# A 2D Fourier transform and a two-layer MLP on one core: loads, tables and low halves as pieces of the written-out order, and the folding of later batches on VectorE

## The chip, the cores and the metric

One NeuronCore of a Trainium2 chip runs the kernel as one program. The metric is the device time of an execution in microseconds. TensorE (PE) multiplies matrices, VectorE (DVE), ScalarE (ACT) and GpSimd (POOL) work element by element, SyncE (SP) issues most of the DMA transfers. Each engine takes its own instructions in order; semaphores join them.

## The reference

The input x has 8 batches of 3008 rows with 256 features. Of each batch the 2D Fourier transform is taken, and its real part goes, row by row, through a two-layer MLP:

```
X = np.fft.fft(np.fft.fft(x, axis=1), axis=2).real        # x: (8, 3008, 256)
h = X.reshape(24064, 256) @ w_in                          # w_in: (256, 2048)
r = np.maximum(h, 0.0)
out = (s * (r * r) + b) @ w_out                           # w_out: (2048, 256)
```

## The kernel before

**What is computed where.** The transform over the features is a matrix on the features, so it is multiplied into w_in once, at the start (`fold_w_in`, pieces "w"). The transform over the 3008 rows is a real transform with many symmetries. Rows that lie symmetrically are added and subtracted first (folding, `load_first`, `load_second` for batch 0, `load` for the others); what remains are eight small sums per batch half, which TensorE makes with cosine and sine tables `dft_sb` (`transform`, L573), and VectorE joins into the spectrum. The spectrum of a batch has 3 blocks of 502 columns.

**Precision.** TensorE's fast format keeps fewer bits, so operands are split into a high part and a low rest: the spectrum into `spec_h` and `spec_l`, the weights into `wd_h`/`wd_l` and `wo_h`/`wo_l`, the activations into `gh` and `gl`. A product is three matmuls (high x high, high x low, low x high).

**A step** is one block of a batch with one of 16 slices of the 2048 hidden features; there are 8 x 3 x 16 = 384. `first_layer` (a piece "L"): six matmuls into two PSUM banks `ab` (L646), three VectorE operations that read them (L651, L654, L655) and make `h`, then relu, square and the cast to `gh` on ScalarE (L656, L657, L666). The low half `gl` = h - gh (L669) is the second part of the same generator (a piece "G"): GpSimd makes it, for some steps of the first block VectorE. `second_layer` (a piece "S"): twelve matmuls on `gh` and `gl` into four banks `po` (L679). After the 16th S of a block, `finish` turns the four banks into results (L696) and stores them. The banks `ab` are four, and the transform takes its PSUM from the same four; `h`, `gh` and `gl` have three buffers each.

**The order is written out by hand.** Two strings of letters say in which order pieces of work are emitted; `_in_order` then ties the instructions of PE, DVE, ACT and POOL to just this order. SP isn't tied, but it also takes its DMA issues in the order of emission. START covers batch 0 and the first 54 S, BATCH is run for each later batch. Letters: "x", "y" fold batch 0; "s", "u" are its transform, phase 0 and 1, in 11 pieces each; "l" folds the next batch, 8 chunks of five operations, one operation a piece (L504, L506, L508, L510, L512); "v", "o" are the next batch's transform; "r" loads a piece of the weights, "a", "b", "e", "f" decode it; "n", "m" are the one feature that stands apart; "t" loads tables. In the pieces of "v", v1 to v7 hold in turn: the first `lf`, matmuls, joining, matmuls, joining, `uv` (L385, L386), the second `lf` (L388, L389, L367); v8 holds the matmuls that need it, v9 to v11 joining, matmuls and joining.

**Before, around the change.** The x tiles of batch 0, the feature table `feat` and two pieces of the weights are issued ahead of the order, in the sequence of LOADS ("xxfxxxwxwxx"); the tables `dft_sb` are issued through GpSimd's own queue (L727). All folding of batches 1 to 7 runs on GpSimd (`LOADS_ON_GPSIMD` names all eight chunks). In BATCH an "L" emits its `gl` at once, and in START "G" is a letter of its own:

```
if what == "L" and step < NB * NBLK * NJ:
    first()
    next(lows.pop(0))
```

The functions that the change touches, and those that call them:

Of the kernel before, what the change touches and what calls it, by code (L numbers as in the profile page):

```python
# [15 lines left out]
P = 128  # L16
NB, S, D, FF = 8, 3008, 256, 2048
# [4 lines left out]
G = 24  # L22
# [12 lines left out]
SPLIT = 754  # L35

LOWS_OF_STEPS_ON_VECTOR = (0, 1, 2, 3, 4, 7, 8, 10, 11, 12, 14)
LOWS_ON_VECTOR = (5,)  # L40
Y_ON_VECTOR = (0, 1, 2, 5)
X_ON_VECTOR = (0, 1, 2, 3, 5, 6, 7)
LOADS_ON_GPSIMD = (0, 1, 2, 3, 4, 5, 6, 7)
SUMS_ON_SCALAR = ()
LOADS = "xxfxxxwxwxx"
WORDS = (
    ("in", 0, 0), ("in", 0, 1), ("in", 1, 0), ("in", 1, 1), ("out", 0), ("out", 1), ("in", 2, 0), ("out", 2),
    ("in", 2, 1), ("out", 3), ("in", 3, 0), ("out", 4), ("in", 3, 1), ("out", 5), ("out", 6), ("out", 7),
)
START = (  # L50
# [7 lines left out]
)  # L58
BATCH = (
# [3 lines left out]
)  # L63

def _unit(num, den):
# [141 lines left out]
def _lay_out_x(x):  # L218

    rows, swap = _rows()
    padded = np.zeros((NB, S + 1, D), np.float32)
    padded[:, :S] = x
    first = np.arange(P)
    second = np.concatenate([[0], D - np.arange(1, P)])
    order = np.stack([np.concatenate([first, second]), np.concatenate([second, first])])
    xq = np.ascontiguousarray(padded[:, rows[..., None], order[swap]])
    xn = np.ascontiguousarray(padded[:, rows, P].transpose(1, 2, 3, 0))  # L230
    return xq, xn

def _in_order(tc):
# [14 lines left out]
def kernel(ctx: ExitStack, tc: tile.TileContext, xq, xn, dft, turn, feat, w_in, w_out, s, b, out):  # L250
    nc = tc.nc
# [4 lines left out]
    stage = ctx.enter_context(tc.tile_pool(name="stage", bufs=2))  # L256
# [4 lines left out]
    act = ctx.enter_context(tc.tile_pool(name="act", bufs=3))  # L261
# [14 lines left out]
    feat_sb = const.tile([P, 2, 2 * P], F32, name="feat_sb")  # L276
# [17 lines left out]
    def load_words(part, pool, tag):  # L294
        raw = pool.tile([P, 512, 2], I32, name="raw", tag=tag)
        src = words(part)
        nc.sync.dma_start(raw.rearrange("p (j d) t -> p j (d t)", j=src.shape[1]), src)
        return raw
# [401 lines left out]
                nc.sync.dma_start(out[su, blk, :, 2 * pm:2 * pm + 2], o)  # L700

    room = spec.tile([P, 2 * NT], F32, name="room", tag="spec_h")
    t_ny = room[:R, 256:512].rearrange("p (c q b) -> p c q b", c=8, q=4)
    nc.sync.dma_start(t_ny, xn)
    nc.sync.dma_start(turn_sb, turn)  # L710
    folded[0] = spare.tile([P, 2, 8, 2 * P], F32, name="cs")
    tiles, raws = [], []
    for what in LOADS:
        if what == "x":
            pool, tag = ((stage, "xt"), (act, "gl"), (act, "gh"))[(len(tiles) + 1) // 3]
            tiles.append(pool.tile([R, 4, D], F32, name="xt", tag=tag))
            nc.sync.dma_start(tiles[-1], xq[0, :, len(tiles) - 1])
        elif what == "w":
            raws.append(load_words(WORDS[len(raws)], act, "h"))
        else:  # L720
            nc.sync.dma_start(feat_sb, feat.rearrange("c p d -> p c d"))
    nc.sync.dma_start(sb_s, s.partition_broadcast(P))
    nc.sync.dma_start(sb_b, b.partition_broadcast(P))

    def tables():
        for ph, leaves in ((0, slice(0, 4)), (0, slice(4, 8)), (1, slice(0, 8))):
            nc.gpsimd.dma_start(dft_sb[:, ph, :, leaves], dft[:, ph, :, leaves])  # L727
            yield

    def load_weights():  # L730
        for part in WORDS[2:]:
            raws.append(load_words(part, stage, "xt"))
            yield

    decoding = []
# [22 lines left out]
    pending, lows = [], []  # L758
# [20 lines left out]
    def second():  # L779
# [6 lines left out]
            finish(su, blk, po)  # L786

    work = {
        "t": tables(), "x": load_first(tiles), "y": load_second(tiles), "r": load_weights(), "a": begin_weights(),
        "b": go_on(), "e": go_on(), "f": go_on(), "w": fold_weights(),  # L790
        "n": nyquist(0, t_ny, room), "m": nyquist(1, t_ny, room),
        "s": transform(0, 0), "u": transform(0, 1), "l": load(1),
# [13 lines left out]
    while step < NB * NBLK * NJ:  # L806
        work = {}
        if su < NB - 1:
            work = {"l": load(su + 1), "v": transform(su + 1, 0), "o": transform(su + 1, 1)}
        for what in BATCH.split():  # L810
            if what == "L" and step < NB * NBLK * NJ:
                first()
                next(lows.pop(0))
            elif what == "S" and pending:
                second()
            elif what in work:
                next(work[what])
        su += 1
    while pending:
        second()  # L820
    _in_order(tc)
# [32 lines left out]
```

## Time and profile before

| | |
|---|---|
| runs | 1632.76, 1634.05, 1635.02 us; median 1634.05 us |
| profiled execution | 1632.94 us, span of its instructions 1631.2 us |
| mean granted TensorE clock | 0.986 of 2.4 GHz |
| GpSimd busy | 1143.4 us, 70% of the span, 842 instructions |
| transfers | 67.41 MB, mean 41 GB/s |
| steps of the two layers | 384, with 1536 x 3 matmuls at L679 and 768 x 3 at L646 |

The profile is of one execution. Matmuls are pipelined, so the mean length of one (0.38 us) is longer than the distance at which they start (0.21 us). A wait is put down to the instruction that came last. The body of the run repeats once per batch.

### The profile page before, as it was taken

How to read it: one execution, taken by the hardware profiler on the slowest of the kernel's cores; microseconds unless marked ns; L12 is line 12 of the kernel's file. 1: busy time of each engine (PE TensorE's matmuls, PEld its weight loads, DVE VectorE, ACT ScalarE, POOL GpSimd, SP SyncE). 2: the span in 40 equal slices, each digit the busy share in tenths (PEclk: the TensorE clock that was granted, in tenths of full speed). 3: DMA queues.
4: the chain of work that ended last, by engine and by line, in shares of the span. 5: the costliest groups of instructions: out<-in, count | busy, mean ns of one | idle time of the engine just before them, and what ended most of it. 6: DMA issues, size and time to landing. Idle time of an engine off the chain costs nothing.

```text
span 1631.2 us, 21931 instructions
## 1 busy us (share of the span) xinstructions
PE 1573.0 (96%) x7526; PEld 1384.5 (85%) x7526; DVE 1128.8 (69%) x1738; ACT 1234.5 (76%) x1311; POOL 1143.4 (70%) x842
## 2 busy tenths in 40 slices
PE   3889999999999999999999999999999999999998
PEld 2568888888888888888888888888888888888887
DVE  7898658757775577756776658765777557775563
ACT  2688687786777778787787877878677777878776
POOL 4647785698557976589766895669855797655554
PEclk8899999999999999999999999999999999999999
DMA  6311110021000210002100110002100021000000
GB/s 177 104 56 61 44 57 10 23 71 45 26 33 17 65 58 4 33 26 65 51 8 26 62 46 35 8 26 71 46 26 32 17 65 42 1 32 8 26 26 26
DMA packets 25316, 67.41 MB, mean 41 GB/s; under 512 B 4915, under 2 KB 9875, under 8 KB 25206
## 3 DMA queue, kind: packets, MB, share of 16 engines
q1 hardware_dynamic: 24934, 64.83, 12.5%
q0 software_dynamic: 272, 1.18, 0.3%
q8 instruction: 60, 0.98, 0.3%
q14 instruction: 50, 0.41, 0.1%
HBM read 41.27 MB, written 24.73 MB: 40 GB/s over the span
## 4 chain that ended last, share of the span: by engine, by line
PE 86%; DVE 8%; ACT 2%; issue 1%; DMA 1%; POOL 1%; SPq 0%; ACTq 0%; DVEq 0%; POOLq 0%
PE po L679 55%; PE ab L646 28%; PE ab L573 3%; DVE uv L385 1%; DVE even L651 1%; DVE lf L388 1%; DVE h L654 1%; DVE h L655 1%; DMA xt<-in_xq 1%; ACT h L657 0%; ACT h L656 0%; DVE uv L386 0%; DVE lf L377 0%; PE ab L338 0%; DMA wny<-wny_dram 0%
## 5 line engine op out<-in xcount | busy, mean ns | idle before, releaser
L669 POOL TENSOR_TENSOR gl<-h,gh 128x1004 fp32r<-128x1004 f32 x373 | 804.7, 2159 | 395.4 <-ACT gh L666 334.7
L656 ACT ACTIVATE h<-h 128x1004 f32<-128x1004 f32 x384 | 398.5, 1038 | 264.7 <-DVE h L655 260.2
L651 DVE SCALAR_TENSOR_TENSOR even<-ebc,wny,ab 128x502 f32<-128x502 f32 x384 | 282.4, 736 | 376.9 <-PE ab L646 358.2
L679 PE MATMUL po<-gh,wo_h 128*128 128x502 f32 (+1 forms) x1536 | 456.6, 379 | 1.5 <-ACT gh L666 1.1
L679 PE MATMUL po<-gh,wo_l 128*128 128x502 f32 (+1 forms) x1536 | 453.1, 377 | 1.3 <-DVE wo_l L273 1.3
L666 ACT CAST gh<-h 128x1004 fp32r<-128x1004 f32 x384 | 395.3, 1029 | 56.6 <-PE po L679 45.5
L657 ACT ACTIVATE h<-h 128x1004 f32<-128x1004 f32 x384 | 399.8, 1041 | 12.2
L679 PE MATMUL po<-gl,wo_h 128*128 128x502 f32 (+1 forms) x1536 | 388.4, 375 | 2.8 <-DVE gl L669 2.8
L679 PEld LDWEIGHTS po<-gh,wo_l 128*128 128x128 f32 x1536 | 292.1, 190 | 37.4 <-DVE wo_l L273 1.6
L679 PEld LDWEIGHTS po<-gh,wo_h 128*128 128x128 f32 x1536 | 290.4, 190 | 38.6 <-issue 1.9
L679 PEld LDWEIGHTS po<-gl,wo_h 128*128 128x128 f32 x1536 | 290.6, 189 | 38.2 <-DVE gl L669 3.2
L654 DVE TENSOR_TENSOR h<-even,ab 128x502 f32<-128x502 f32 x384 | 260.2, 678 | 77.8 <-POOL gl L669 27.3
L646 PE MATMUL ab<-spec_h,wd_h 128*128 128x502 f32 x768 | 296.1, 386 | 8.4 <-DVE even L651 6.5
L646 PE MATMUL ab<-spec_l,wd_h 128*128 128x502 f32 x768 | 291.2, 379 | 0.0
L646 PE MATMUL ab<-spec_h,wd_l 128*128 128x502 f32 x768 | 289.9, 377 | 0.0
L655 DVE TENSOR_TENSOR h<-even,ab 128x502 f32<-128x502 f32 x384 | 257.9, 671 | 0.0
L646 PEld LDWEIGHTS ab<-spec_h,wd_h 128*128 128x128 f32 x768 | 145.7, 190 | 33.1 <-DVE even L651 9.1
L646 PEld LDWEIGHTS ab<-spec_h,wd_l 128*128 128x128 f32 x768 | 146.6, 191 | 18.1
L646 PEld LDWEIGHTS ab<-spec_l,wd_h 128*128 128x128 f32 x768 | 146.0, 190 | 17.8 <-issue 0.8
L696 DVE TENSOR_SCALAR o<-po,sb_s,bias 128x502 f32<-128x502 f32 x94 | 68.7, 793 | 12.4 <-PE po L679 12.3
L561 POOL TENSOR_TENSOR spec_l<-o,spec_h 128x368 fp32r<-128x368 f32 (+3 forms) x80 | 61.6, 791 | 18.1 <-ACT spec_h L559 14.7
L573 PEld LDWEIGHTS ab<-dft_sb,lf 96*128 96x128 f32 x384 | 51.4, 195 | 25.3 <-DVE lf L388 20.1
(94 smaller groups left out, 819.3 us busy)
## 6 DMA issues: line engine op xcount, KB each, us to landing
xt<-in_xq SPq DMA_DIRECT2D x64, 384.0 KB
out<-o SPq DMA_DIRECT2D x46, 502.0 KB
raw<-in_w_in SPq DMA_DIRECT2D x8, 512.0 KB
raw<-in_w_out SPq DMA_DIRECT2D x8, 512.0 KB
ebc<-e_dram SPq DMA_DIRECT2D x16, 251.0 KB
ebc<-e_dram SPq DMA_DIRECT2D x8, 126.0 KB
out<-o SPq DMA_DIRECT2D x4, 251.0 KB
ebc<-e_dram SPq DMA_DIRECT2D x8, 125.0 KB
```

The lines of the kernel that those rows point to most:

```text
L561: nc.gpsimd.tensor_sub(lo, src, hi.bitcast(F32))
L573: nc.tensor.matmul(ps[:, kind, i], src[:, i, kind * P:(kind + 1) * P], dft_sb[:, ph, kind, leaf + i], start=True, stop=True,)
L646: nc.tensor.matmul(beside(ps[kind]), w[:, kind, fj], in_turn(m[:, kind]), start=i == 0, stop=i == 2)
L651: nc.vector.scalar_tensor_tensor(beside(even), in_turn(ebc), wny[:, j:j + 1], beside(ps[0]), op0=ALU.mult, op1=ALU.add)
L654: sub(h[:, 1], even, ps[1])
L655: add(h[:, 0], even, ps[1])
L656: nc.scalar.activation(h, h, AF.Relu)
L657: nc.scalar.activation(h, h, AF.Square)
L666: nc.scalar.copy(gh_halves, h)
L669: engine.tensor_sub(gl_halves, h, gh_halves.bitcast(F32))
L679: nc.tensor.matmul(beside(po[2 * pm + dh][:, :n]), l[:, j, dh * P:(dh + 1) * P], in_turn(r[:, pm])[:, :n // 2], start=start and i in (0, 2 ...
L696: nc.vector.tensor_scalar(o[:, dh], po[2 * pm + dh][:, :NT], *args, ALU.mult, ALU.add)
```

## The change

The loads of batch 0 and of the constants become pieces ("X", "c"), as the tables ("t") already were. The tables go through SyncE's queue. All 16 pieces of weights are loaded by "r". In BATCH, "G" is now a letter of its own, as in START; what is left of the low halves is emitted after the last batch's string. `LOADS_ON_GPSIMD` is empty, so `load` takes VectorE for all chunks of batches 1 to 7. START and BATCH are written anew.

```diff
-LOADS_ON_GPSIMD = (0, 1, 2, 3, 4, 5, 6, 7)
+LOADS_ON_GPSIMD = ()
-LOADS = "xxfxxxwxwxx"
...
 START = (
-    "t t x a r n y x r x x x s y n y b n x x s y x y s s a x s e s f b s s e a u t s a b e f w s r s b u u y e a f "
-    "y r b f w w w w a e y f L b r r e a u L a G b r L e b r e f G a L b G a f e b w r S S f S r f u w w w L G e a "
-    "a m L G b b e S e f S L r a L r G r b e G m f m a L r u S f L G L G G S L S b u e a S S G u f u w b f w w e u "
-    "u a G f S L L b G e S G f L L S l L l G G S L l l l G L S l l G S L l G L l G S G l L G S L S l S l L l l G l "
-    "S L S L l S L G S G S l G l L l L G G l l l l G S L S v G L S L l l G L l l G S l l S l l S L L G S L l l L l "
-    "S G l L G S G l L G G v l l S v l L S G L S S L S v G l v S G v v L L S o G L v G o G v G S L S L v G S v L o "
-    "S G L o L G o G S L S S L L G S G G o L S G G L L S L S S G o o G G o o o S"
+    "X X n X X x X X r X y t X x y x a r x t y r x x r c s s a b e x b t x x e a f n b s e f w r y s s w f n s s a "
+    "a s u u b e s b u e y r y a s f s b w e w f w r a L y y r b a L r G L e b e f r G S a L b e G f f G u c S u f "
+    "r S w w w a b w a m L S L r m u b e e G f a L G r L b e G a S f S f L r L b G G m e r f a G L S b e r u S w w "
+    "u w f a u a L u L b G e b u S f G L e S S f L S G G L L G l S L l G G S L S S l L L S l l G S L l G G S l L S "
+    "l L G l S l G G l l l L l l S L G S G l G L l l l S L G G l S l L S l G l L l L v S v G S l v l L S G l L G L "
+    "G l G l l S L l S S L L l S l L S L l G L l l v S v l l l G L l G S G S S G o S v L G L G v G G S L L G S S v "
+    "G o v L v o S G L S v o L S o G L G L G o S S S G L L S S o G L G G L S o o S L G L G G S L G o S o"
 )
 BATCH = (
-    "l l L S S S l l L L S l l l L l L S l L L l S l L l S L l l S l S L L l l S L l l L l S S l l l L l L l S l S "
-    "S S L v l S l l L l S L l L v S L l l l l l v l S l v S l v L l L S L S L v v L S S v v L S L L S v L S S S o "
-    "L S v L L o S o L S o L S o L S L L o S L S L L o S S S o L S o L S L L S S L L S o L S o L S S"
+    "l l L G S l S S l l L G L G G l S l L l l l L S G l L G S G l l l L G l l S L l G l L S l l L S l S G L G L l "
+    "S S G l L v G L v l l S L S G l G L l l S l L S G l L G v l S G L S l L G v l l l G L S G G v S l S l L S l l "
+    "l v L G v S L G S L S L S G v L G G S L G S v L o S o G L o v G v S G L S G L L S L o G o L S o S L G L o S G "
+    "S L L S G G G L o S G G S G o S L L S S L L S L G o G G G S o L S L G L S S G S G"
 )
...
-    for what in LOADS:
-        if what == "x":
-            pool, tag = ((stage, "xt"), (act, "gl"), (act, "gh"))[(len(tiles) + 1) // 3]
+
+    def load_x():
+        for c in range(8):
+            pool, tag = ((stage, "xt"), (act, "gl"), (act, "gh"))[(c + 1) // 3]
             tiles.append(pool.tile([R, 4, D], F32, name="xt", tag=tag))
-            nc.sync.dma_start(tiles[-1], xq[0, :, len(tiles) - 1])
-        elif what == "w":
-            raws.append(load_words(WORDS[len(raws)], act, "h"))
-        else:
-            nc.sync.dma_start(feat_sb, feat.rearrange("c p d -> p c d"))
-    nc.sync.dma_start(sb_s, s.partition_broadcast(P))
-    nc.sync.dma_start(sb_b, b.partition_broadcast(P))
+            nc.sync.dma_start(tiles[-1], xq[0, :, c])
+            yield
+
+    def load_constants():
+        nc.sync.dma_start(feat_sb, feat.rearrange("c p d -> p c d"))
+        yield
+        nc.sync.dma_start(sb_s, s.partition_broadcast(P))
+        nc.sync.dma_start(sb_b, b.partition_broadcast(P))
+        yield
 
     def tables():
         for ph, leaves in ((0, slice(0, 4)), (0, slice(4, 8)), (1, slice(0, 8))):
-            nc.gpsimd.dma_start(dft_sb[:, ph, :, leaves], dft[:, ph, :, leaves])
+            nc.sync.dma_start(dft_sb[:, ph, :, leaves], dft[:, ph, :, leaves])
             yield
 
     def load_weights():
-        for part in WORDS[2:]:
-            raws.append(load_words(part, stage, "xt"))
+        for i, part in enumerate(WORDS):
+            raws.append(load_words(part, *((stage, "xt") if i > 1 else (act, "h"))))
             yield
...
             if what == "L" and step < NB * NBLK * NJ:
                 first()
+            elif what == "G" and lows:
                 next(lows.pop(0))
...
         su += 1
+    for low in lows:
+        next(low)
     while pending:
         second()
```

## Rows read from the trace of the kernel before

**Rows 1.** The page, busy time by engine: us, share of the span, instructions.
```profile
PE 1573.0 (96%) x7526; PEld 1384.5 (85%) x7526; DVE 1128.8 (69%) x1738; ACT 1234.5 (76%) x1311; POOL 1143.4 (70%) x842
```

**Rows 2.** Windows: length; PE, PEld, DVE, ACT, POOL busy us; clock; DMA share, GB/s.
```profile
0.00:10.00 10.00, 0.00 (x0) 0.00 (x0) 3.95 (x11) 1.28 (x1) 4.34 (x15) 1.00 0.79 199
10.00:20.00 10.00, 2.01 (x5) 0.69 (x6) 7.96 (x18) 1.95 (x7) 4.78 (x11) 1.00 1.03 290
400.00:420.00 20.00, 18.35 (x87) 15.87 (x86) 19.28 (x25) 12.84 (x14) 11.74 (x7) 0.91 0.20 72
1075.00:1174.00 99.00, 99.00 (x477) 88.42 (x476) 59.58 (x92) 76.93 (x78) 86.12 (x68) 1.00 0.15 44
1075.00:1268.00 193.00, 191.31 (x925) 170.51 (x924) 132.44 (x204) 149.50 (x154) 142.50 (x98) 0.99 0.12 37
1180.00:1200.00 20.00, 18.88 (x88) 16.57 (x89) 17.48 (x27) 14.41 (x16) 10.19 (x7) 0.91 0.13 53
```

**Rows 3.** Waits of VectorE to 150 us: us in total, times, longest.
```profile
DVE xt L521 <- DMA xt<-in_xq: 7.8, 2, 5.9
DVE even L651 <- DMA wny<-wny_dram: 4.6, 2, 2.4
```

**Rows 4.** Operations on `uv` from 400 us: count, ns min/median/max, first and last start.
```profile
L385 DVE TENSOR_TENSOR uv<-cs x6: 3612/3626/3655, 400.2 to 1368.5; 96x512 f32<-96x512 f32 x6
L386 DVE TENSOR_TENSOR uv<-cs x6: 674/676/677, 403.8 to 1372.0; 96x512 f32<-96x512 f32 x6
```

**Rows 5.** Timeline near 400 us: start, us, operation, idle time before it.
```profile
399.04 4.25 POOL L669 TENSOR_TENSOR gl<-h,gh 128x1004 fp32r<-128x1004 f32 x2
...
400.23 3.61 DVE L385 TENSOR_TENSOR uv<-cs 96x512 f32<-96x512 f32 x1
...
404.04 2.40 POOL L669 TENSOR_TENSOR gl<-h,gh 128x1004 fp32r<-128x1004 f32 x1 [0.75 <-ACT gh L666]
...
404.36 2.35 DVE L388 TENSOR_TENSOR lf<-uv 96x256 f32<-96x256 f32 x1
406.64 0.41 DVE L389 TENSOR_TENSOR lf<-uv 96x256 f32<-96x256 f32 x1
...
406.77 1.24 PE L573 MATMUL ab<-dft_sb,lf 96*128 96x96 f32 x8 [1.65 <-DVE lf L388]
```

**Rows 6.** Waits of TensorE from 260 us on.
```profile
PE ab L573 <- DVE lf L388: 10.0, 6, 1.7
```

**Rows 7.** Timeline near 193 us.
```profile
193.28 5.81 DVE L377 TENSOR_TENSOR lf<-cs 96x256 f32<-96x256 f32 x1
...
194.60 4.22 POOL L669 TENSOR_TENSOR gl<-h,gh 128x1004 fp32r<-128x1004 f32 x2
...
199.80 0.78 PE L646 MATMUL ab<-spec_h,wd_h 128*128 128x502 f32 x1 [2.97 <-DVE even L651]
```

**Rows 8.** Lines of VectorE, 1075 to 1268 us: count, busy us, mean ns.
```profile
L651 DVE SCALAR_TENSOR_TENSOR even<-ebc,wny,ab 128x502 f32<-128x502 f32 x48 | 35.3, 735 | 48.7 <-PE ab L646 46.9
...
L655 DVE TENSOR_TENSOR h<-even,ab 128x502 f32<-128x502 f32 x48 | 32.2, 672 | 0.0
L696 DVE TENSOR_SCALAR o<-po,sb_s,bias 128x502 f32<-128x502 f32 x12 | 8.8, 793 | 0.4 <-PE po L679 0.4
```

**Rows 9.** Lines of GpSimd in the same stretch.
```profile
L504 POOL TENSOR_TENSOR xt<-xt 96x512 f32<-96x512 f32 x8 | 10.4, 1302 | 0.0
...
L506 POOL TENSOR_TENSOR xt<-xt 96x256 f32<-96x256 f32 x8 | 5.9, 732 | 0.4
```

**Rows 10.** The chain of waits near 222 us: start, us, what.
```profile
222.18 2.54 PE po L679 x12
224.72 1.27 PE ab L646 x6
```

**Rows 11.** Lines of ScalarE from 1075 to 1268 us.
```profile
L657 ACT ACTIVATE h<-h 128x1004 f32<-128x1004 f32 x48 | 50.0, 1041 | 1.5
```

**Rows 12.** Timeline of VectorE in the opening.
```profile
6.97 0.28 DVE L407 TENSOR_TENSOR room<-room 96x128 f32<-96x128 f32 x1
```

More of the change, by code (lines that the diff above doesn't have):

```diff
@@ L788 @@
     work = {
-        "t": tables(), "x": load_first(tiles), "y": load_second(tiles), "r": load_weights(), "a": begin_weights(),
+        "X": load_x(), "c": load_constants(), "t": tables(), "x": load_first(tiles), "y": load_second(tiles), "r": load_weights(), "a": begin_weights(),
         "b": go_on(), "e": go_on(), "f": go_on(), "w": fold_weights(),
```

## The prediction

> **What bounds the kernel now.** I read the page first: TensorE is busy for 1573 of 1631.2 us, the next engine, ScalarE, for 76% [rows 1]. So only time in which TensorE stands, or runs at half clock, can be won. Windows of 10 and 20 us, and then the waits, show three places that hold it.
>
> The opening: in the first 10 us TensorE does nothing, in the next 10 it works 2.01 us [rows 2], and while VectorE folds batch 0, rebuilds the weights and feeds the first steps, it is filled unevenly until about 140 us. VectorE is the engine without air there; its two largest waits, for x and for `wny`, sum to 12.4 us, of which 5.9 is the landing of the first x [rows 3].
>
> One stall per batch: at 406.77 TensorE waits 1.65 us for `lf` L388. Upstream, `uv` L385 needs 3.61 us and ends just after a pair of `gl` does (399.04 + 4.25 = 403.29), though its twin L386 needs 0.68. L388 takes 2.35 us, against 0.41 for L389 with the same shape, and again ends with a `gl` (404.04 + 2.40) [rows 4, 5]. It repeats: the six L385 from 400.2 to 1368.5 us lie 193.7 us apart and all take 3.6 us [rows 4], and TensorE waits for L388 six times, 10.0 us in all [rows 6]. Behind four of the six the granted clock falls as well, to 0.91 over 20 us, 1.8 us each; the rows of the first and the last of them stand for the four [rows 2].
>
> One hold near 193 us: `lf` L377, of the shape that takes 0.41 us when free, takes 5.81. It starts while GpSimd folds and ends after two `gl` that follow without a gap (194.60 + 4.22 = 198.82). TensorE waits 2.97 us behind it, and its next matmul lasts 0.78 us, against 0.38 at full clock [rows 7].
>
> So a VectorE operation with two SBUF inputs doesn't run beside a GpSimd operation: it waits for its end, and for the next one's if that follows at once. Those with an input in PSUM (L651, L655) keep their length [rows 8].
>
> The Trainium skill says this in "SBUF — State Buffer", "SBUF: two separate sides": the pair of ports that VectorE and GpSimd share is an exclusive lock, held for a whole instruction, also against a VectorE operation with two SBUF inputs. The trace agrees for one instruction and goes beyond it in L377, which was held through several. It speaks against this change, as all 280 moved operations are of that kind; the time by it is rival 2.
>
> **The change part by part.**
>
> *Folding batches 1 to 7 on VectorE.* A batch has 8 chunks of 5 operations. GpSimd loses 10.4 us for L504 and about 5.9 us for each of the four like L506, 34 us a batch [rows 9]. VectorE gets 8 x (0.68 + 4 x 0.41) = 18.5 us, by the free L386 and L389 [rows 4, 5].
>
> Has VectorE room? I add up the new BATCH from its start to its 23rd S, which covers all 40 `l` and v1 to v7. VectorE: 23 L of 0.735 + 2 x 0.672 = 2.08 us, 47.8; one group of results, 4 x 0.79 = 3.2; the 13 operations of the v pieces at 0.41 to 0.68, 6.3; the folds, 18.5; in all 75.8 us [rows 8]. TensorE: 23 x (1.27 + 2.54) = 87.6 us, its two small groups of the transform left out [rows 10]. So 11.8 us are free for holds. The 40 `l` stand in 26 runs with an L between them or a v, so each run may be held 0.45 us on average before VectorE sets the pace. Before, GpSimd was busy for 86.1 of 99 us in this stretch and VectorE for 59.6 [rows 2]: the load is turned round, with a lower peak.
>
> How long will a run be held? From nothing to a whole `gl`, 2.13 us (half of the pair's 4.25) [rows 5]. I take 0.2, by the phase: ScalarE needs 3 x 1.04 = 3.1 us between the last `h` of a step and its `gl` [rows 11], and most `l` stand directly behind an L, when the step's own `gl` can't have begun. The `gl` of the step before ends 3.1 + 2.13 us behind its own `h`, and a step is 3.81 us, so at most 1.42 us of it are left when VectorE is punctual, and less the later VectorE is. With 26 x 0.2 = 5 us this half holds 81 of 88 us: free for TensorE, which has a lead of 3 to 5 steps. I add 2 us over the run for single collisions (0 to 12).
>
> *The stalls that go.* The new order puts four S and three L between v7, which makes `lf`, and v8, which needs it: 14.0 us, where the old one has two S and one L, 6.4 us [rows 10]. And GpSimd, without the folds, seldom has two operations back to back. Gain 6 x 1.65 + 4 x 1.8 = 17.1 us; from 8, if a hold of `lf` merely shrinks, to all of it. Late next would be the PSUM bank that v2 holds until v3, now over four L in place of one: an L then finds three banks, and VectorE must have read the first half of the step before within some 3 us. At its load that holds.
>
> The hold near 193: gone with the folds on GpSimd, 2.97 us and, as behind the other stalls, about 1.7 of clock: 4.7 us (0 to 4.7).
>
> *The price in START.* Batch 1 is folded beside the late opening. From S28 to S36 the new START gives VectorE 10 L (20.8), 16 `l` (7.4), v3 and v5 (2.2) and a group of results (3.2), 33.6 us, and TensorE 8 x 2.54 + 10 x 1.27 = 33.0. No room there; a lead of 4 to 5 steps takes some 4 us of lag. I take +3 (0 to 10).
>
> *Loads and tables as pieces, tables through SyncE.* SyncE's queue now holds x ahead of everything, and feat, the tables and most weights later. VectorE's second wait for x, 7.8 - 5.9 = 1.9 us [rows 3], came with feat and two tables ahead of or beside the third x. And n now stands ahead of the first fold, so that 0.5 us of its work (L407, 0.28, and the smaller L408) falls into the first 5.9 [rows 12]. New on SyncE are three table issues. The first stands behind seven x and a word, 3.4 MB: at the 290 GB/s of the second 10 us [rows 2] through by some 14 us, while `s1` has 13 us of VectorE's work ahead of it behind the first landing, so about 19. feat and the third table stand behind a word that waits for the slot of the second x, freed early, by y2. GpSimd loses three issues in an opening where it is busy for less than half [rows 2]: 0, and if that cover were gone, what they took of it. Gain 2.4 (from -6, if SyncE's line runs late, to 6.5, the two waits without the first landing).
>
> *The rest of the opening.* By S13 either order has given VectorE the same pieces, so another sequence moves only its waits; 0.6, within the bounds just given.
>
> *G as pieces in BATCH.* GpSimd keeps only `gl` and `spec_l`, 142.5 - 34 = 108.5 of 193 us [rows 2], and takes them as they come. 0; were that cover gone, a `gl` behind two `spec_l` is under 2 us late, inside the lead.
>
> Sum, from the profiled execution's 1632.9 us (span 1631.2; 1.1 under the runs' median 1634.05): -17.1 - 4.7 - 3.0 + 2 + 3 = -19.8, so 1613; on the median's level 1614.
>
> **Rivals.**
>
> 1. *The stall changes place.* Holds of `uv`, `o`, `lf` and the folds still cost TensorE a stop in each batch, and the clock with it. For: `gl` alone was what L385 and L388 sat behind at 400 us, and `gl` remains. Against: the 14 us between v7 and v8. If all 17.1 us come back, 1634 - 3 - 4.7 + 5 = 1631; with half of them 1623.
>
> 2. *VectorE becomes the bound of the folding half (slower).* Each run of `l` meets a running `gl`, and GpSimd takes the port again between runs. It decides from 0.45 us of hold per run on, in six batches and, with as many runs, in START. At 0.6 us: 26 x 0.15 x 7 = 27 us, 1641; at 0.9: 82 us, 1696. The worst, a whole `gl` for each run, is 26 x 1.68 x 7 = 306 us. For: all six L385 were held 2.9 us. Against: they met two `gl` in a row behind a GpSimd that had folded until then, and L386 and L389, second in their run, weren't held at all [rows 4, 5].
> The skill's page named above gives the same end: whoever comes second blocks fully. What it leaves open is how often VectorE comes second.
>
> 3. *The opening suffers.* Tables, feat and weights in one line behind slot waits make `s` or `u` late: 6 us worse, with the stalls still gone 1623. If the order packs the opening instead, 10 us better: 1604.
>
> That the change doesn't do what it says would be folds left on GpSimd; `LOADS_ON_GPSIMD = ()` excludes it.
>
> **How the numbers follow.** The forecast (stalls gone, VectorE keeps up) with rival 3's milder forms, 1602 to 1622, gets 0.60; rival 1, 1622 to 1637, 0.22; rival 2, from 1637 on, 0.18. The predicted time is 1614. The range 1598 to 1641 takes in rival 1 and the mild end of rival 2, and leaves out the rest of it and a still better opening; the forecast's own range is 1602 to 1622. A measurement of this kernel can tell 0.2% (3.3 us) from no change: faster 0.60 and 0.15 of rival 1, 0.75; same 0.07; slower 0.18.
>
> **What would show it.** Right: no wait of TensorE for L388 after 260 us, a granted clock of 1.0 in all windows there, GpSimd near 56% and VectorE near 80% of the body, L506 to L512 on VectorE at a mean below 0.6 us, and a batch of 190 to 191 us in place of 193.7. Wrong: those means above 1 us, TensorE waiting for L651 or L655 in the folding half, VectorE above 95% there, or VectorE's waits in the first 150 us grown.

## The result, and the profile after

The changed kernel takes 1594.07 us (median of four runs, 1593.48 to 1594.51) against 1633.99 us: a ratio of 0.9756, interval 0.9739 to 0.9773. The forecast was 1614 us and the range 1598 to 1641; the sign was right, the gain of 39.9 us is twice the 19.8 that were forecast, and the time lies below the range.

The line numbers fell by 14 (L651 is now L637, L388 is L374, L573 is L559); the folds L504 to L512 are now L490 to L498. The page of the changed kernel, busy time by engine [rows 1]:

```profile
PE 1555.3 (98%) x7526; PEld 1377.2 (87%) x7526; DVE 1235.8 (78%) x2018; ACT 1233.0 (77%) x1311; POOL 920.8 (58%) x559
```

Its windows, the first two as in [rows 2], then the folding part of one batch and the whole of that batch:

```profile
0.00:10.00 10.00, 0.00 (x0) 0.00 (x0) 4.60 (x14) 2.12 (x6) 2.39 (x16) 1.00 0.77 199
10.00:20.00 10.00, 2.03 (x9) 1.89 (x10) 9.76 (x25) 1.23 (x2) 2.55 (x3) 1.00 1.03 278
1065.00:1158.00 93.00, 93.00 (x452) 83.17 (x451) 76.47 (x129) 75.35 (x75) 53.61 (x25) 1.00 0.19 58
1065.00:1255.10 190.10, 190.10 (x930) 170.17 (x928) 148.99 (x245) 149.58 (x155) 111.07 (x59) 1.00 0.12 38
```

TensorE is never idle in that batch, at full clock; the list of its waits from 260 us to the end, where [rows 6] had six stalls, has no entry. VectorE and GpSimd have changed places, 78% and 58%. Operations on `uv` and `lf` [rows 4]:

```profile
L371 DVE TENSOR_TENSOR uv<-cs x6: 686/689/689, 375.9 to 1326.4; 96x512 f32<-96x512 f32 x6
L374 DVE TENSOR_TENSOR lf<-uv x6: 647/648/657, 379.1 to 1329.6; 96x256 f32<-96x256 f32 x6
```

`uv` takes 0.69 in place of 3.6 us, and six of them lie (1326.4 - 375.9) / 5 = 190.10 us apart, where it was 193.66. The folds on VectorE, 420 to 1400 us (count, busy us, mean ns):

```profile
L490 DVE TENSOR_TENSOR xt<-xt 96x512 f32<-96x512 f32 x40 | 41.5, 1039 | 0.0
L494 DVE TENSOR_TENSOR xt<-xt 96x256 f32<-96x256 f32 x40 | 24.9, 622 | 0.0
L496 DVE TENSOR_TENSOR cs<-xt 96x256 f32<-96x256 f32 x40 | 18.6, 464 | 1.0
L492 DVE TENSOR_TENSOR xt<-xt 96x256 f32<-96x256 f32 x40 | 18.4, 460 | 0.5
L498 DVE TENSOR_TENSOR cs<-xt 96x256 f32<-96x256 f32 x40 | 16.6, 414 | 0.0
```

The means sum to 3.00 us a chunk; free it would be 0.68 + 4 x 0.41 = 2.32. So 0.68 x 8 = 5.4 us of hold a batch. Counted with only an L, v or o between them, as the forecast words it, the `l` of the new BATCH stand in 20 runs and not in 26 (26 takes any letter between); it is 0.27 us for each of the 20, or 0.21 for each of 26.

Where the 39.5 us of span went is read from the stores of results on SyncE (start, us). Before:

```profile
151.10 1.77 SPq L700 DMA_DIRECT2D out<-o  x2
217.25 1.78 SPq L700 DMA_DIRECT2D out<-o  x2
284.35 1.75 SPq L700 DMA_DIRECT2D out<-o  x2
...
1625.52 1.80 SPq L698 DMA_DIRECT2D out<-o  x4
```

After:

```profile
138.52 1.75 SPq L686 DMA_DIRECT2D out<-o  x2
200.06 1.78 SPq L686 DMA_DIRECT2D out<-o  x2
265.26 1.75 SPq L686 DMA_DIRECT2D out<-o  x2
...
1586.71 1.80 SPq L684 DMA_DIRECT2D out<-o  x4
```

The first block comes 12.6 us earlier; the second gains 4.6 (61.54 against 66.15 us), the third 1.9, all after it 19.7, the tail 0.7. The third block's 1.9 us is almost no stall: in these windows of before and then of after TensorE is idle for 0.33 us and not at all, and after has nine matmuls fewer there, which fall into the next stretch.

```profile
217.20:284.30 67.10, 66.77 (x337) 59.33 (x336) 51.81 (x82) 51.42 (x55) 46.31 (x30) 1.00 0.10 32
```
```profile
200.00:265.20 65.20, 65.20 (x328) 58.59 (x327) 56.40 (x89) 46.59 (x49) 36.21 (x20) 1.00 0.11 33
```

### The profile page after: what moved, and what is told of

Its sections match the earlier page's. It is cut to its first block, busy times and chain, and to the rows that moved or that the text cites. A ratio compares the mean times of both kernels' runs of the same rounds, so it can differ in the third digit from the quotient of the medians.

```text
span 1591.7 us, 22023 instructions
## 1 busy us (share of the span) xinstructions
PE 1555.3 (98%) x7526; PEld 1377.2 (87%) x7526; DVE 1235.8 (78%) x2018; ACT 1233.0 (77%) x1311; POOL 920.8 (58%) x559
## 4 chain that ended last, share of the span: by engine, by line
PE 94%; DVE 3%; DMA 1%; ACT 0%; issue 0%; POOL 0%; SPq 0%; ACTq 0%; DVEq 0%; POOLq 0%
PE po L665 60%; PE ab L632 30%; PE ab L559 3%; DMA raw<-in_w_in 1%; DMA feat_sb<-in_feat 1%; DVE gl L655 0%; DVE even L637 0%; PE ab L324 0%; DVE h L640 0%; DVE h L641 0%; DVE cs L301 0%; DVE aux L301 0%; SPq L700 0%; DVE cs L300 0%; DVE o L682 0%
## 5 line engine op out<-in xcount | busy, mean ns | idle before, releaser
L637 DVE SCALAR_TENSOR_TENSOR even<-ebc,wny,ab 128x502 f32<-128x502 f32 x384 | 281.7, 734 | 227.9 <-PE ab L632 218.4
L665 PEld LDWEIGHTS po<-gh,wo_h 128*128 128x128 f32 x1536 | 287.2, 189 | 35.4 <-DVE o L682 0.7
L632 PE MATMUL ab<-spec_h,wd_h 128*128 128x502 f32 x768 | 292.3, 381 | 6.1 <-ACT spec_h L545 2.8
L490 DVE TENSOR_TENSOR xt<-xt 96x512 f32<-96x512 f32 x56 | 59.3, 1059 | 0.0
```

Source lines behind the costliest of these rows:

```text
L490: engine.tensor_add(t[:, 0::2], t[:, 0::2], t[:, 1::2])
L632: nc.tensor.matmul(beside(ps[kind]), w[:, kind, fj], in_turn(m[:, kind]), start=i == 0, stop=i == 2)
L637: nc.vector.scalar_tensor_tensor(beside(even), in_turn(ebc), wny[:, j:j + 1], beside(ps[0]), op0=ALU.mult, op1=ALU.add)
L665: nc.tensor.matmul(beside(po[2 * pm + dh][:, :n]), l[:, j, dh * P:(dh + 1) * P], in_turn(r[:, pm])[:, :n // 2], start=start and i in (0, 2 ...
```

## The experiments: engine and order in the batches

"Old" and "new" are the orders of before and after. Ratios are to the kernel before, on the same chip. E1, E2 and E4 came out slower than either theory expected.

**E1. The old order, folds on VectorE** (from before).

```diff
-LOADS_ON_GPSIMD = (0, 1, 2, 3, 4, 5, 6, 7)
+LOADS_ON_GPSIMD = ()
```

> The kernel before with one edit: all folding of batches 1 to 7 on VectorE, both orders as they were. Theory 1 (the engine: the hold of uv and lf comes from a GpSimd that folds beside its gl, so taking the folds away removes the stalls in any order): the six stalls go (6 x 3.56 = 21 us by the batch lengths 193.66 before and 190.10 after) and the hold near 193 us too (4.6): about 1609 us. Theory 2 (the order: the stalls go because four S and three L stand between v7 and v8 and not two S and one L; the old order puts up to six folds in a row, and VectorE collides): the stall at L388 stays or another takes its place: 1626 to 1650 us.

1663.66 us, ratio 1.0185 [1.0169, 1.0202]: slower by 30. TensorE's waits from 260 us:

```profile
PE ab L646 <- DVE x L582: 15.8, 6, 2.6
PE ab L646 <- DVE even L651: 6.3, 7, 1.3
PE ab L646 <- DVE h L655: 4.1, 7, 0.6
```

The timeline of one of the six:

```profile
391.87 2.30 POOL L669 TENSOR_TENSOR gl<-h,gh 128x1004 fp32r<-128x1004 f32 x1 [1.95 <-ACT gh L666]
...
392.08 2.63 DVE L504 TENSOR_TENSOR xt<-xt 96x512 f32<-96x512 f32 x1
...
394.95 2.13 POOL L669 TENSOR_TENSOR gl<-h,gh 128x1004 fp32r<-128x1004 f32 x1 [0.78 <-ACT gh L666]
...
395.56 1.81 DVE L506 TENSOR_TENSOR xt<-xt 96x256 f32<-96x256 f32 x1
...
398.54 0.55 DVE L582 TENSOR_TENSOR x<-t,ab 128x384 f32<-128x384 f32 x1
...
399.23 0.76 PE L646 MATMUL ab<-spec_h,wd_h 128*128 128x502 f32 x1 [2.63 <-DVE x L582]
```

Two folds (free 0.68 and 0.41) are each held to the end of a `gl`; behind them on VectorE stands the joining `x`, which frees the PSUM bank of a v piece, and TensorE waits for the bank. TensorE's wait for `lf` L388 is gone, others have its place.

**E2. The new order, folds on GpSimd** (from after).

```diff
-LOADS_ON_GPSIMD = ()
+LOADS_ON_GPSIMD = (0, 1, 2, 3, 4, 5, 6, 7)
```

> The kernel after with one edit: all folding of batches 1 to 7 on GpSimd again, the new order kept. Theory 1 (engine): uv and lf are held by gl and folds again, VectorE is late, the stalls and the hold come back in some form: 1594 + 21 + 5, about 1612 to 1620 us. Theory 2 (order): the 14 us between v7 and v8 hide a hold of some 5 us: 1594 to 1598 us.

1662.35 us, ratio 1.0176 [1.0161, 1.0191]: slower by 28. The last fold, L498, isn't done when v6 wants it; `uv` and what VectorE waited for ahead of it:

```profile
L371 DVE TENSOR_TENSOR uv<-cs x6: 2607/2607/2609, 389.4 to 1396.7; 96x512 f32<-96x512 f32 x6
...
  POOL cs L498: 30.1, 6
```

TensorE then waits for VectorE, from 260 us on:

```profile
PE ab L632 <- DVE even L637: 29.0, 12, 4.5
```

So the engine alone costs 30, the order alone 28, and both together win 40. All of E2's loss lies in the batches. Its stores of the first and the third block:

```profile
139.49 1.24 SPq L686 DMA_DIRECT2D out<-o  x2
...
266.04 1.75 SPq L686 DMA_DIRECT2D out<-o  x2
```

With the folds still on GpSimd, the new START reaches the third block at 266.04 us, where before has 284.35 and after 265.26: up to there the order with its loads wins 18.3 us without the change of engine. The engine without the order (E1) stores its first block 5.0 us late (156.12) and its third 3.3 late (287.63). From the third store to the end of the span the four kernels need 1346.9 (before), 1374.7 (E1), 1395.1 (E2) and 1326.4 us (after): in the batches the engine alone costs 28, the order alone 48, and both together win 20. There the gain belongs to neither part; in START it belongs to the order, with the new loads.

**E3. The new START, the old BATCH** with its folds on GpSimd.

```diff
 BATCH = (old)
-        engine = nc.gpsimd if c in LOADS_ON_GPSIMD else nc.vector
+        engine = nc.gpsimd if su > 1 else nc.vector
...
-            elif what == "G" and lows:
                 next(lows.pop(0))
```

> The kernel after with the old BATCH (gl emitted with its L) and the folding of batches 2 to 7 on GpSimd; START, loads and tables stay new. If the parts add, this keeps what was won up to the 48th S (19.1 us by the results of block 3: 284.35 before, 265.26 after) and gives back the 20.4 behind it: 1634 - 19 = 1615 us, with six TensorE waits for lf L388 as before (10.0 us in all). Rival: what the opening gives is partly the body's (leads at the seam): 1600 to 1608, or the body's stalls grow: above 1620 us.

1613.74 us, ratio 0.9879 [0.9864, 0.9894]. The six stalls are back, as in [rows 6] (line numbers are 15 lower):

```profile
PE ab L558 <- DVE lf L373: 10.0, 6, 1.7
```

START is worth 20, BATCH with its change of engine 20, and they add.

**E4. The old kernel, only v8 and v9 moved behind more steps.**

```diff
-... v6 v7 L S S v8 v9 L S L L S v10 ...
+... v6 v7 L S S L S L v8 v9 L S v10 ...
```

> The kernel before with one edit in BATCH: v8 and v9 stand one S and two L later (then three S and three L lie behind v7 and not two S and one L), folds stay on GpSimd. Theory 2 (order, spacing): the six waits for lf L388 go and with them 6 x 3.56 = 21 us: about 1613 us. Theory 1 (engine): uv still takes 3.6 us and lf 2.35, VectorE stays behind, the wait shows at the next L (for even L651 or an ab bank): 1624 to 1634 us.

1649.61 us, ratio 1.0100 [1.0083, 1.0117]. No wait for `lf` is left, but a larger one, with `uv` still held for 3.66 us:

```profile
PE ab L646 <- DVE even L651: 15.1, 6, 2.5
```

The distance between v7 and v8, which the forecast gave as the reason, isn't enough by itself, at the three S and three L tried here: what VectorE loses behind the held `uv` shows at the next thing that TensorE needs of it.

**E12. Low halves emitted with their step** in BATCH (from after).

```diff
-            elif what == "G" and lows:
                 next(lows.pop(0))
```

> The kernel after with one edit: in BATCH the low half is emitted at once with its step again, as in the kernel before; the rest of the new order stays. The term of the prediction: nothing, as GpSimd has only gl and spec_l left and takes them as they come: 1593 to 1596 us. Rival: the place of G among the spec_l decides whether an S finds its gl: 1600 us or more.

1594.91 us, ratio 0.9762 [0.9747, 0.9776]: G as a piece of BATCH is worth nothing that can be measured.

## The experiments: who holds whom

**E10 and E11. More work on GpSimd behind each `gl`** from batch 1 on (from after); both overwrite the feature table, which is no longer used then.

```diff
+        if su > 0:
+            f = feat_sb.rearrange("p a d -> p (a d)")
+            nc.gpsimd.tensor_sub(f, f, f)        # E10
+            for _ in range(2):                   # E11 instead
+                nc.gpsimd.memset(f, 0.0)
```

> The kernel after with one addition: from batch 1 on, GpSimd runs one more operation with two SBUF inputs (512 columns, about 1.3 us) behind each gl, on a table that is no longer needed. GpSimd goes from 58% to some 85%. Theory of rival 2 (the hold decides): the folds are held more than the 0.45 us per run that VectorE can bear in the folding half, and TensorE waits there: 1620 to 1680 us. Against it (the folds fall into the same gaps): 1594 to 1600 us.

> The kernel after with one addition: from batch 1 on, GpSimd runs two memsets of 512 columns behind each gl, operations without an SBUF input (about 1 us for the two, an estimate). If only operations that read SBUF hold VectorE, the folds stay as short as in the kernel after and the time is 1594 to 1598 us. If any GpSimd operation holds VectorE, or if the delay of gl itself costs, it goes with the run of the extra operation with two inputs: above 1610 us.

E10: 1682.08 us, ratio 1.0294 [1.0279, 1.0310]. E11: 1592.95 us, ratio 0.9752 [0.9738, 0.9767], the same as after. Both load GpSimd alike, E10 to 78%, E11 to 79%. Two of the folds and the added operation, 420 to 1400 us, and TensorE's wait, in E10:

```profile
L496 DVE TENSOR_TENSOR cs<-xt 96x256 f32<-96x256 f32 x39 | 54.7, 1403 | 1.0
...
L492 DVE TENSOR_TENSOR xt<-xt 96x256 f32<-96x256 f32 x39 | 43.9, 1125 | 0.5
```
```profile
L658 POOL TENSOR_TENSOR feat_sb<-feat_sb 128x512 f32<-128x512 f32 x231 | 272.1, 1178 | 0.0
```
```profile
PE ab L632 <- DVE even L637: 52.0, 18, 5.2
```

In E11 (there is no wait of TensorE):

```profile
L492 DVE TENSOR_TENSOR xt<-xt 96x256 f32<-96x256 f32 x40 | 20.1, 502 | 0.5
L496 DVE TENSOR_TENSOR cs<-xt 96x256 f32<-96x256 f32 x40 | 19.0, 475 | 1.0
```
```profile
L659 POOL MEMSET feat_sb<- 128x512 f32 x496 | 260.8, 526 | 14.3
```

In E10 the five folds' means sum to 5.62 us a chunk, 3.3 over free, or 26.4 us a batch. That is rival 2: over the 11.8 us that the forecast found free in a batch it makes 14.6, and 87.6 us in the six batches that are folded beside the added work; 88 were measured. In E11 they sum to 3.30, a hold of 7.8 us a batch, inside those 11.8, and this load of GpSimd, which reads nothing from SBUF, costs nothing. The Trainium skill, "SBUF — State Buffer", "SBUF: two separate sides", says of an operation with two SBUF inputs that it locks only against a GpSimd operation that reads SBUF; E10 and E11 agree.

## The experiments: the opening

The first store is the measure: 151.10 us before, 138.52 after. It is read from one execution of each kernel. Kernels with the old START and the old loads alike (before, E4) have it at 151.10 and 151.81, and with the new START and folds on VectorE up to there (after, E3, E10, E11, E12) at 138.52, 139.76, 138.05, 137.71 and 141.37. So a difference of some 3 us in it says nothing by itself; the median of the total has to stand beside it.

**E5. Tables through GpSimd's queue**, the rest as after: `nc.gpsimd.dma_start(dft_sb...)`.

> The kernel after with one edit: the three table transfers are issued through GpSimd's queue again, at the same places of the order. Theory 3 (the opening gained because VectorE's waits for wny, for a ScalarE copy and for decoded words went, by the sequence of the pieces): the tables land before s1 either way; 1593 to 1596 us. Theory 4 (the opening gained by its transfers: x in front, tables through SyncE): 1598 us or more.

1595.34 us, ratio 0.9767 [0.9753, 0.9782]; first store 138.77: no difference worth the name.

**E6. The old sequence of loads**, the rest as after.

```diff
-START = "X X n X X x X X r X y t X ... c ..."
+START = "X X c X X X r X r X X c n x y t ..."
```

> The kernel after with one edit: x, feat and the first two words are issued ahead of everything in the old sequence (x x feat x x x word x word x x, then s and b); the rest of the new order stays. Theory 3: VectorE waits for the third x again, 1.9 us, and the tables land a little later: 1595 to 1598 us. Theory 4: most of the 12.6 us that the first block won go: 1600 to 1607 us.

1598.99 us, ratio 0.9787 [0.9772, 0.9801]: 4.9 us lost. The first store, at 141.00, is that of the fastest of the four runs (1596.07 us) and lies inside the spread above.

**E7. The old order of the engines' pieces with the new loads** (X, c, t and r through SyncE).

```diff
-START = "t t x a r n y x r x x x s ..."
+START = "X X X X X X r X t X r t x a r n y x r c t x x x s ..."
```

> The kernel before with the new loads alone: six x, a word, x, table, x, word, table ahead of the old order, then feat and the third table behind two more words, all through SyncE; the engines' pieces keep the old sequence, the folds stay on GpSimd. Theory 3: only the 1.9 us of the second wait for x go: 1631 to 1633 us. Theory 4: 8 to 12 us go: 1622 to 1626 us. If a table or feat now lands late: above 1635 us.

1632.17 us, ratio 0.9991 [0.9981, 1.0001]; first store 149.72. The loads alone are worth 1.4 us, which isn't clear of noise. E7 and E2 have the same loads and the same engine for the folds, and differ up to the first store in the order of START alone: 149.72 against 139.49, so the order is worth 10.2 us there.

**E8. The old kernel with `wny` brought back earlier**: w6 behind e5, w10 behind f13, w11 behind w10, w12 behind u9.

> The kernel before with one edit in START: w6 stands behind e5, and w10, w11, w12 move up behind f13, w10 and u9, so that the columns of wny for the second and the fourth quarter of the features are written, and read back, earlier. VectorE waited 4.6 us for them. Theory 3: these 4.6 us go, since VectorE is the engine that bounds the opening: 1629 to 1630.5 us. Theory 4 (transfers) or a rival by which the wait was covered anyway (another wait comes last): 1633 to 1635 us.

1635.18 us, ratio 1.0012 [1.0003, 1.0021]. The wait of 4.6 us [rows 3] is gone, and VectorE waits elsewhere:

```profile
DVE wd_l L273 <- ACT wd_h L272: 6.2, 3, 2.8
```

**E9. The old kernel with TensorE kept busy**: seven more matmuls, whose sums nobody reads, between s4 and s8.

```diff
+        for i in range(7):
+            nc.tensor.matmul(spare_ps[:, :480], ..., start=True, stop=True)
```

> The kernel before with one edit in START: seven matmuls of 480 columns on data that is there, whose sums nobody reads, fill TensorE between s4 and s8, where it stood for 7.6 us and then ran at half clock (four matmuls at L338 took 3.67 us there, 1.9 us at full clock). Theory 5 (the clock took part in the opening: s10, and the ScalarE copy behind it for which VectorE waited 2.3 us, stood behind these slow matmuls): granted clock 1.0 from 30 to 40 us, the first step some 2 us earlier, 1630 to 1632 us. Rival (VectorE's own work and its other waits set the pace, the clock is only a sign of it): 1633 to 1635 us.

1634.11 us, ratio 0.9999 [0.9989, 1.0009]. The window from 30 to 40 us before, and then in E9:

```profile
30.00:40.00 10.00, 6.59 (x20) 4.29 (x21) 8.09 (x16) 2.15 (x4) 3.77 (x4) 0.53 0.24 61
```
```profile
30.00:40.00 10.00, 10.00 (x41) 5.94 (x39) 8.66 (x17) 3.42 (x7) 2.89 (x3) 1.00 0.33 82
```

TensorE had worked for 5.18 of the 10 us ahead of that window before, and for all of them in E9. The clock is full where it was at half, and the first block (store at 151.06) comes no earlier: from 30 to 40 us the low clock cost nothing. From 40 to 50 us it is as low as before (0.78 against 0.81), so what it costs there is not shown.

**E13 to E18. Orders cut and joined.** All have the new loads, folds on VectorE and the new order behind the 16th S; pieces that the first part has already emitted are left out of the second.

```diff
-START = new
+START = new up to L1, old up to S16, new           # E13
+START = old up to L1, new                          # E14
+START = old up to S16, new                         # E15
+START = new up to S5, old up to S16, new           # E16
+START = E16 with l3 to l7 behind S16, as in new    # E17
+START = E17 with f13, w10, w11, w12 as in new      # E18
```

> The new kernel, but between the first L and the 16th S the pieces stand in the order of before (first L to first block), and then the new order again. First result stored at 138.52 us in the new kernel, 149.72 in the old order with the new loads; VectorE idles 6.0 us less up to the first `even` in the new one. Theory (the two halves of the opening each give about half, and add): the gain up to the first step stays, 149.7 - 6 = 143.7 us for the first store, total 1594 + 5 = 1599. Rival A (all is won after the first step, the lead is eaten by whatever comes late anyway): store at 149 to 150, total 1605. Rival B (all is won ahead of the first step): store at 138 to 140, total 1594 to 1596.

> The reverse: up to the first L the pieces in the order of before (with the new loads), then everything as in the new kernel. Theory (halves add): first `even` about 6 us later than in the new kernel (53.5 in place of 47.5), store at 138.5 + 6 = 144.5, total 1600. Rival A (all won after the first step): store at 138.5 to 140, total 1594 to 1596. Rival B (all won ahead of it): store at 149 to 150, total 1605.

> The new kernel with the order of before (new loads) up to the 16th S, and the new order from there: the base for the two others. All theories on the opening: store at 149.7, total 1594 + 11 = 1605, since what follows the first block was found to add to it. If the later part takes the delay back (its folds of batch 1 start earlier against TensorE), less than 1605; if TensorE's late start meets the folds of batch 1 worse, more.

> The new order up to the fifth S, then the order of before up to the 16th, then the new one. Theory (the time after the first step is won evenly, by VectorE's idle time): about half of the later half's 6 us stays, store at 141 to 142, total 1597. If the stretch between the first step and the fifth S holds it all: store at 138.5 to 139.5, total 1594 to 1595. If it is the stretch from the fifth S on: store at 143.7, as with the order of before from the first step on, total 1599.

> The kernel with the new order up to the fifth S and the old one from there to the 16th, but the five folding pieces l3 to l7, which the old order has ahead of the 16th S, stand where the new order has them. With them ahead the first block was stored at 149.09 us, 10.6 later than in the new kernel, of which VectorE's idle time is 4.3 and its busy time 6.2 us. Theory (the folds of batch 1, free 2.3 us, and what they are held, are the 6.2 us): store at 149.1 - 6 = 143, total 1598 to 1600 (some of it moves behind the first block). Rival (they only fill idle time, and what is longer are other operations held by GpSimd): store at 147 to 149, total 1603.

> The last one, and the pieces w10, w11 and w12, that bring the row `wny` back from memory, and f13, which they follow, stand where the new order has them. Theory (the 2.6 us for which VectorE waited for `wny`, and TensorE's late start behind it, are what is left of its idle time): store 2.6 us earlier than in the last one, about 140.5, total 1596 to 1597. Rival (as in the old order, another wait takes its place): the same store and total as the last one within 1 us.

| | time, us | ratio and interval | first store, us |
|---|---|---|---|
| E15 | 1609.53 | 0.9859 [0.9844, 0.9874] | 154.58 |
| E13 | 1606.49 | 0.9837 [0.9820, 0.9853] | 151.20 |
| E16 | 1604.02 | 0.9825 [0.9810, 0.9839] | 149.09 |
| E17 | 1598.62 | 0.9789 [0.9774, 0.9803] | 143.01 |
| after | 1594.07 | 0.9756 [0.9739, 0.9773] | 138.52 |
| E14 | 1601.46 | 0.9809 [0.9794, 0.9823] | 146.15 |
| E18 | 1602.98 | 0.9812 [0.9796, 0.9829] | 150.06 |

E15 to after is a chain in which one stretch at a time takes the new order: the part up to the first step gives 3.4 us, from there to the fifth S 2.1, the five folds moved behind the 16th S 6.1, the rest of the sequence 4.5; 16.1 in all, and the total follows it to within 0.7 us (3.0, 2.5, 5.4, 4.6 by the medians; the first two are about as large as the intervals). None of the theories that put the gain into one place holds; E17's, that the five folds are worth 6 us, came out as forecast. The parts don't add freely: the first is worth 7.6 us in front of the new order (E14) and 3.4 in front of the old, where VectorE comes earlier and then waits for TensorE. Its waits of that kind to 160 us in E13, and then in E15:

```profile
DVE even L637 <- PE ab L632: 3.6, 2, 1.9
...
DVE x L567 <- PE ab L559: 1.9, 1, 1.9
```
```profile
DVE even L637 <- PE ab L632: 0.8, 1, 0.8
...
DVE x L567 <- PE ab L559: 0.3, 1, 0.3
```

The chain is longer than the 12.6 us that were won because its start is worse than the kernel before. E15 and E7 have the same order up to the 16th S and the same loads, and only the engine of the folds differs up to the first store: 154.58 against 149.72. Folds on VectorE in the old places cost 4.9 us (5.0 in E1), and the five folds' move mostly takes this back.

The five folds' free time is 2.3 us; in E16 (the window to the first store, then one of its folds from 125 us on, held for 2 us) they cost 6.1:

```profile
0.00:149.00 149.00, 112.19 (x485) 83.47 (x485) 129.97 (x223) 95.97 (x144) 79.76 (x123) 0.96 0.35 102
```
```profile
L498 DVE TENSOR_TENSOR cs<-xt 96x256 f32<-96x256 f32 x1 | 2.4, 2366 | 0.0
```

against E17:

```profile
0.00:143.00 143.00, 108.72 (x479) 81.96 (x480) 126.38 (x218) 93.31 (x142) 75.89 (x123) 0.98 0.36 103
```

VectorE is busy for 3.6 us more in E16, and idle for 2.4 more (19.0 against 16.6). E18 lost 4.4 us in the median where 2.6 were to be won (7.1 at the first store, but its profile is of the slowest of its four runs); its pieces of "w" came ahead of what ScalarE makes for them:

```profile
DVE wd_l L259 <- ACT wd_h L258: 7.7, 1, 7.7
```

## Why the prediction was wrong

**The step that failed: "The rest of the opening. By S13 either order has given VectorE the same pieces, so another sequence moves only its waits; 0.6, within the bounds just given."** With the loads' 2.4 it made 3.0 us; measured are 12.6, and 10.2 in place of the 0.6 for the order alone (E7 against E2). The pieces are nearly the same at S13 (the new order has one L, one G and one fold more), but the same pieces are not the same time. The windows to the first store, before and after:

```profile
0.00:151.10 151.10, 112.43 (x479) 84.22 (x480) 126.96 (x216) 92.39 (x142) 78.95 (x130) 0.91 0.34 99
```
```profile
0.00:138.50 138.50, 107.38 (x479) 82.39 (x480) 123.78 (x218) 93.82 (x143) 75.30 (x123) 0.98 0.37 107
```

VectorE's idle time, 151.1 - 127.0 = 24.1 us before, is 14.7 after, and its busy time falls by 3.2 us, though two folds of batch 1 are added, as operations that were held in the old order run free in the new one (L389, 1.50 us before, is L375 with 0.41). Of the 9.4 us of idle time, 7.2 are the two waits of [rows 3] themselves: those for x and for `wny` were 12.4 us, and after has these two, and none for `wny`:

```profile
DVE room L393 <- DMA room<-in_xn: 2.7, 1, 2.7
DVE xt L507 <- DMA xt<-in_xq: 2.5, 1, 2.5
```

I had counted 3.0 us of the 7.2. The other 2.2, and the 3.2 of busy time, lay outside what I had looked at. I had bounded the gain by the two waits of [rows 3], 6.5 us without the first landing; the bound should have been the idle time of the engine that I had myself called the one without air, 24.1 less the 5.9 of the landing. Of what was forecast, the other half of rival 3 comes nearest: that the order packs the opening, 10 us better.

Term by term, forecast against measured:

| term | forecast | measured |
|---|---|---|
| six stalls for `lf` | -17.1 | -20.4 (4 x 3.8 + 2 x 2.6) |
| hold near 193 us | -4.7 | -4.6 |
| opening | -3.0 | -12.6 |
| price of the folds in START | +3 | 0 |
| single collisions | +2 | 0 |
| remainder | | -1.9 |
| sum | -19.8 | -39.5 |

- **Stalls.** That they would go was right, and the size was short by 3.3 us. Behind the six waits before, TensorE goes on at 406.77, 600.60, 794.56, 987.27, 1181.12 and 1375.04 us. The third of these distances, behind a stall at which the granted clock stayed full (1.00 in the 6 us from 794 us), is 192.71 us; the other four, behind those at which it fell (0.72 in such 6 us), are 193.83 to 193.96. Against 190.10 after, a stall made a batch 2.6 us longer without the fall of the clock and 3.8 with it. So the clock cost 1.2 us and not 1.8, and nearly 1 us more than the wait of 1.65 went in every batch, a term that the forecast lacked; where it goes is not isolated. E4 shows that a longer distance to v8 alone would not have done it, E1 that the change of engine alone would not.
- **Hold near 193 us.** Right in place and near in size: the second block took 66.15 us before (65.21 in E4, with the same START) and takes 61.54. The reason given, folds no longer on GpSimd, is one of two: the block takes 62.26 us in E1, where only they are gone, and 61.87 in E2, where only the order is new.
- **Two prices that never came.** TensorE is busy for all of 200 to 265 us, where START folds batch 1, and waits nowhere behind 260 us. I had let a lead of 4 to 5 steps take some 4 us of lag and still taken +3; what bore the lag is not shown. The prices exist: in the old order the folds cost 5 us at the first store (E1, E15), and with 26 us of hold a batch 88 us in all (E10).
- **Holds of the folds.** 26 x 0.2 = 5.2 us a batch was assumed, 5.4 measured; the count of runs was wrong (20, as above), which leaves the 11.8 us that were free in a batch as they are. For the reason given, that most `l` stand where no `gl` runs, E1 speaks: the same folds in the old order have means of 0.64 to 1.32 us, and that kernel is 30 us slower than before.
- **Tables and G as pieces.** 0 and 0, as forecast (E5, E12). Loads: 1.4 (E7, not clear of noise) to 4.9 us (E6), depending on what stands behind them, against 2.4.
- **What would show it.** GpSimd 58% (56), VectorE 78% (80), batch 190.1 us (190 to 191), clock 1.00, no wait for L388: as forecast. L494 misses the mean of 0.6 us by 0.02.

What stays open: which of the moved pieces between the fifth and the 16th S make the last 4.5 us (E17 to after); and where nearly 1 us goes behind each stall beside the wait and the clock.

## What to carry to other kernels

Where one engine paces an opening, bound what a new order can win by that engine's whole idle time and the time for which its operations are held, not by its largest named waits; a wait taken away alone (E8, E18) came back elsewhere in the chain that feeds the engine. In a body that repeats, move work between VectorE and GpSimd together with its place in the order: either half of this change alone lost 28 to 30 us. Ask of each stretch apart which half it needs: the opening needed only the order with its loads. Put VectorE's operations with two SBUF inputs where GpSimd's next read can't have begun yet, and price the rest by the time they are held.

## What was not expected of the hardware

A GpSimd operation that only writes (memset, 526 ns, 496 of them in 980 us) left VectorE's two-input operations nearly as they were (3.30 us a chunk against 3.00), while one of 1178 ns with two inputs raised their sum to 5.62. And a TensorE at half clock for most of 10 us (0.53 granted) cost nothing: with 1.00 granted in the same window (E9) the first block was stored at 151.06 us in place of 151.10. A stall of TensorE of 1.65 us, on the other hand, made a batch 2.6 us longer where the granted clock stayed full and 3.8 where it fell.
